# First Fourier axis of a mixing block folded once more: rows s paired with 272 - s, in four regrouped row tiles

## The chip, the cores and the metric

The kernel runs on one core of a Trainium2 chip. The metric is the device time of one execution in microseconds: 313.57 us is the median of 3 runs before the change (313.29 to 314.12). The profile that is shown is of one such execution, with a span of 312.0 us.

## The reference

A cross attention between 512 tokens `x` and 32 state rows (8 heads of 64 columns, batch 8) gives 544 rows of 512 columns for each batch. On these a Fourier mixing block works: the real part of a two-dimensional DFT is added, the rows are normalised, and a two-layer network (512 to 2048 to 512) is applied.

```python
def _attn_ref(x, state):                      # x (8, 8, 512, 64), state (8, 8, 32, 64)
    scores = scale * x @ state^T              # softmax over the 32 states
    xread = softmax(scores) @ state           # 512 rows
    scores2 = scale * state @ x^T             # softmax over the 512 tokens
    sread = softmax(scores2) @ x              # 32 rows
    return concatenate([xread, sread], axis=2)

def _moe_ref(x, w_ch1, w_ch2):                # x (8, 544, 512): heads side by side
    X = np.fft.fft(np.fft.fft(x, axis=1), axis=2)
    u = x + np.real(X)
    un = (u - mean(u)) / sqrt(var(u) + 1e-6)  # over the last axis
    return u + np.maximum(un @ w_ch1, 0) @ w_ch2
```
(shortened)

## The kernel before

The first Fourier axis has 544 rows s. A cosine is the same for s and 544 - s, a sine changes sign, so the kernel adds row 544 - s to row s first, and 288 table rows are left for the matmul (`NM = 288`: outputs 1 to 287 and 0). Rows come as three tiles: rows 1 to 128 and 129 to 256, each with its mirrored partner, and the *low* tile of 32 rows (257 to 287, and 0), which is read by a small attention read of its own. The columns (second axis) are folded twice, which gives four quarters j of 128 columns. The parts that matter, with cuts marked `...`:

```python
def load_x(b):
    if b < 2:                                       # 1 KB pieces: 4 rows of a head
        v = xs.rearrange("p (h r) -> p h r", h=H)
        xb = x[b].rearrange("h (p i) d -> p h (i d)", i=4)
        ...
    # b >= 2: rows by tile, pieces of 64 float32 = 256 bytes
    for ps, si, rows in ((slice(32, 128), 2, xb[288:384]), (slice(0, 128), 0, xb[1:129]),
                         (slice(0, 128), 1, xb[129:257]), (slice(0, 128), 3, xb[384:512]),
                         (slice(0, 31), 2, xb[257:288]), (slice(31, 32), 2, xb[0:1])):
        nc.sync.dma_start(out=v[ps, si], in_=rows)

def xread(c0, rev, name, o, ...):                   # attention read of 128 rows
    # two matmuls of 260 columns on TensorE, then reciprocal and product on VectorE

def low():
    xread(256 - 32 * bq, False, "xlp", XL[pq, 0:512], pq)

def fold_rows(k, eng=nc.vector):
    eng.tensor_add(Sm[:, k], XF[:, k], XR[:, k])                          # L518
    eng.tensor_add(XE[:, k, 0:256], Sm[:, k, 0:256], Sm[:, k, 512:256:-1])  # L519
    eng.tensor_copy(XE[:, k, 256:257], Sm[:, k, 256:257])                 # L520
    yield

def fold():                                         # on VectorE
    next(fold_rows(slice(1, 2) if b < 2 else slice(0, 2)))
    nc.vector.tensor_add(XQ[:, 0], XE[:, :, 0:128], XE[:, :, 256:128:-1]) # L529
    nc.vector.tensor_sub(XQ[:, 1], XE[:, :, 0:128], XE[:, :, 256:128:-1]) # L530
    nc.vector.tensor_copy(XN[:, :, 0:1], XE[:, :, 128:129])
    nc.vector.tensor_sub(XO[:, 0:2, 1:256], Sm[:, :, 1:256], Sm[:, :, 511:256:-1])
    nc.vector.tensor_sub(XQ[:, 2], XO[:, :, 0:128], XO[:, :, 256:128:-1]) # L533
    nc.vector.tensor_add(XQ[:, 3], XO[:, :, 128:0:-1], XO[:, :, 128:256]) # L534

second = [                                          # the reads of a batch, woven into the stream
    lambda: xread(256, True, "xrp", XR[:, 0, 1:513]),
    sread if b < 2 else sread_by_head,              # overwrites XR[0:32, 0]
    None if b > 1 else lambda: (low(), fold_low_early()),
    lambda: xread(0, False, "xfp", XF[:, 0, 0:512], apart=(b == 0)),
    low if b > 1 else lambda: next(fold_rows(slice(0, 1), nc.gpsimd)),
    lambda: xread(128, False, "xfp", XF[:, 1, 0:512], apart=(b == 0)),
    (lambda: (fold_low(True), fold_low(False))) if b > 1 else None,
    lambda: (xread(384, True, "xrp", XR[:, 1, 1:513]), fold()),
]

def over_s(j):                                      # first axis, quarter j of the columns
    p = qt("gp")
    tab = cos if j < 2 else sin
    for c in range(3):                              # three row tiles, 288 outputs
        nc.tensor.matmul(p[:, 0:NM], lhsT=XQ[:, j, c, :], rhs=tab[c],
                         start=(c == 0), stop=(c == 2 and j != 2))
    if j == 2:
        for c in range(3):
            nc.tensor.matmul(p[:, 0:NM], lhsT=XN[:, c, :], rhs=cos[c], start=False, stop=(c == 2))
    ...                                             # copy to G by ScalarE
```

The eight batches overlap: while the network of batch b runs (`layer1` writes `ph`, `layer2` writes `po`), the reads of batch b+1 and then its transform are woven into TensorE's stream at fixed shares of the stretch:

```python
def weave(*streams):    # sorts the steps of all streams by lo + (hi - lo) * (i + 0.5) / len(steps)
...
streams.append((reads_next, 0, 0.34))
streams.append((transform(b + 1), 0.47 if b == 1 else 0.4, 0.77 if b == 3 else 0.8))
```

Each engine works its instructions off in program order. The `warm` matmuls at the start compute nothing that is used.

Of the kernel before, what the change touches and what calls it, by code (L numbers as in the profile page):

```python
# [12 lines left out]
F32 = mybir.dt.float32  # L13
# [17 lines left out]
def kernel(  # L31
# [43 lines left out]
    nc.gpsimd.iota(lt, pattern=[[1, NM]], base=1, channel_multiplier=0)  # L75
# [3 lines left out]
    for hh in range(4):  # L79
        nc.gpsimd.iota(pi_[32 * hh:32 * hh + 32, 2:3], pattern=[[0, 1]], base=257, channel_multiplier=1)  # L80
# [28 lines left out]
    def load_x(b):  # L109
        xs = wk.tile([128, 4 * dm], F32, name="xs", tag="xs")  # L110
        xs_of[b] = xs
        if b < 2:
            v = xs.rearrange("p (h r) -> p h r", h=H)
            xb = x[b].rearrange("h (p i) d -> p h (i d)", i=4)
            n = 2 if b == 0 else 4
            for h in range(0, H, n):
                queue = nc.scalar if b == 0 and h in (0, 4) else nc.sync
                queue.dma_start(out=v[:, h:h + n, :], in_=xb[:, h:h + n, :])
            return
        v = xs.rearrange("p (i h d) -> p i h d", i=4, d=D)  # L120
        xb = x[b].rearrange("h s d -> s h d")
        for ps, si, rows in (
            (slice(32, 128), 2, xb[288:384]),
            (slice(0, 128), 0, xb[1:129]),
            (slice(0, 128), 1, xb[129:257]),
            (slice(0, 128), 3, xb[384:512]),
            (slice(0, 31), 2, xb[257:288]),
            (slice(31, 32), 2, xb[0:1]),
        ):
            nc.sync.dma_start(out=v[ps, si], in_=rows)  # L130

    def cast_x(b, copy=nc.gpsimd.tensor_copy, lo=0, hi=H):
        if b < 2:
            copy(xin_bufs[b % 2][:, :, 1 + D * lo:1 + D * hi].rearrange("p i (h d) -> p h i d", d=D),
                 xs_of[b].rearrange("p (h i d) -> p h i d", i=4, d=D)[:, lo:hi])
        else:
            copy(xin_bufs[b % 2][:, :, 1:513], xs_of[b].rearrange("p (i c) -> p i c", i=4))  # L137
# [38 lines left out]
    CL = singles.tile([128, 4, NM], BF16, name="CL")  # L176
    SL = singles.tile([128, 4, NM], BF16, name="SL")
    cast_x(0, nc.scalar.copy, 0, 2)
    cast_x(0, nc.scalar.copy, 2, 4)
    cast_x(0, lo=4, hi=6)  # L180
    cast_x(0, lo=6, hi=8)

# [10 lines left out]
    XE, XO = singles.tile([128, 3, 257], F32, name="XE"), singles.tile([128, 3, 257], F32, name="XO")  # L193
    XQs, XNs = two("XQ", [128, 4, 3, 128]), two("XN", [128, 3, 128])
# [3 lines left out]
    CT = singles.tile([128, 2, NM], BF16, name="CT")  # L198
    ST = singles.tile([128, 2, NM], BF16, name="ST")
# [4 lines left out]
    cl1 = gen1[:, 2048:2048 + NM // 2].bitcast(BF16)  # L204
    sl1 = gen1[:, 2560:2560 + NM // 2].bitcast(BF16)
# [18 lines left out]
    nc.vector.memset(lt[:, NM - 1:NM], 0)  # L224
    nc.vector.tensor_copy(pf, pi_)
    nc.vector.scalar_tensor_tensor(pf[:, 2:3], in0=pf[:, 2:3], scalar=float(NM), in1=pf[:, 2:3], op0=ALU.is_lt, op1=ALU.mult)
    pn = singles.tile([128, 3], F32, name="pn")
    nc.vector.tensor_scalar(pn, in0=pf[:, 0:3], scalar1=1.0 / Stot, scalar2=None, op0=ALU.mult)
    f1, q1 = turn(NM, Stot, lt, [0, 1, 2], gen1)
# [22 lines left out]
    def sines():  # L252
        w = 2.0 * PI / Stot * shrink
        nc.scalar.activation(CT, q1[:, 0:2, :], AF.Sin, bias=halfpi, scale=-w)
        nc.scalar.activation(ST, f1[:, 0:2, :], AF.Sin, bias=0.0, scale=w)
        nc.scalar.activation(CL[0:32, 0, :], q1[0:32, 2, :], AF.Sin, bias=halfpi[0:32], scale=-w)
        nc.scalar.activation(SL[0:32, 0, :], f1[0:32, 2, :], AF.Sin, bias=0.0, scale=w)

    def low_tables(hh):
        pq = slice(32 * hh, 32 * hh + 32)  # L260
        nc.gpsimd.tensor_copy(CL[pq, hh, :], cl1[pq])
        nc.gpsimd.tensor_copy(SL[pq, hh, :], sl1[pq])

    def more_sines():
        w = 2.0 * PI / dm * shrink
        nc.scalar.activation(TE[:, 0:128], q2_[:, 0:128], AF.Sin, bias=mhalfpi, scale=w)
        nc.scalar.activation(TE[:, 128:256], q2_[:, 0:128], AF.Sin, bias=sg[:, 2:3], scale=sg[:, 3:4])
        nc.scalar.activation(TO[:, 0:128], f2[:, 256:384], AF.Sin, bias=0.0, scale=w)
        nc.scalar.activation(TO[:, 128:256], f2[:, 256:384], AF.Sin, bias=0.0, scale=sg[:, 3:4])
        nc.scalar.activation(TE[:, 256:384], q2_[:, 128:256], AF.Sin, bias=mhalfpi, scale=w)  # L270
        nc.scalar.activation(TE[:, 384:512], q2_[:, 128:256], AF.Sin, bias=sg[:, 2:3], scale=sg[:, 3:4])
        nc.scalar.activation(TO[:, 256:384], f2[:, 128:256], AF.Sin, bias=0.0, scale=w)
        nc.scalar.activation(TO[:, 384:512], f2[:, 128:256], AF.Sin, bias=0.0, scale=sg[:, 3:4])

    def last_sines():
        w = 2.0 * PI / Stot * shrink
        nc.scalar.activation(cl1, q1[:, 2, :], AF.Sin, bias=halfpi, scale=-w)
        nc.scalar.activation(sl1, f1[:, 2, :], AF.Sin, bias=0.0, scale=w)
# [9 lines left out]
    def clears(i):  # L288
        nc.gpsimd.memset(XFs[i][:, :, 512:514], 0.0)
        nc.gpsimd.memset(XRs[i][:, :, 0:514:513], 0.0)  # L290
        nc.gpsimd.memset(XLs[i][:, 512:514], 0.0)
        if i == 0:
            nc.gpsimd.memset(XE[:, 2, :], 0.0)
            nc.gpsimd.memset(XO[:, 2, :], 0.0)
            nc.gpsimd.memset(XO[:, 0:2, 0:257:256], 0.0)
        nc.gpsimd.memset(XNs[i].rearrange("p a b -> p (a b)"), 0.0)

# [6 lines left out]
    nc.gpsimd.memset(CL.rearrange("p a b -> p (a b)").bitcast(F32), 0.0)  # L304
    nc.gpsimd.memset(SL.rearrange("p a b -> p (a b)").bitcast(F32), 0.0)
# [3 lines left out]
    def more_loads():  # L309
        nc.gpsimd.tensor_copy(gate[:, 0:1], XQs[0][:, 3, 0, 0:1])  # L310
# [7 lines left out]
    def last_loads():  # L318
        for hh in range(1, 4):
            low_tables(hh)  # L320
# [37 lines left out]
    def attend(b):  # L358
# [4 lines left out]
        XQ, XN = XQs[b % 2], XNs[b % 2]  # L363
# [19 lines left out]
        def turn_x(g):  # L383
# [5 lines left out]
            for k in range(2):  # L389
                for si in range(4):  # L390
                    o = k * 512 + si * 128
                    nc.tensor.transpose(p[:, o:o + 128], xin[:, si, 1 + 128 * (2 * g + k):129 + 128 * (2 * g + k)], ident)
            (nc.vector.tensor_copy if g == (b == 0) else nc.scalar.copy)(
                xT[:, 2 * g:2 * g + 2, :], p.rearrange("p (a b) -> p a b", b=S))
# [18 lines left out]
        def scores_t(g):  # L413
            p = qt("eTp")
            for i in range(4):
                x0 = 128 * i
                for cols, rows in ((slice((i - 1) % 4, 285 if i == 0 else 288, 4), slice(x0 + (i == 0), x0 + 72)),
                                   (slice(287, 288), slice(0, 1)) if i == 0 else (None, None),
                                   (slice(291 - i, S, 4), slice(x0 + 127, x0 + 71, -1))):
                    for hp in range(2 if cols else 0):  # L420
                        nc.tensor.matmul(p[:, cols], lhsT=sT[:, 2 * g + hp, :], rhs=xT[:, 2 * g + hp, rows],  # L421
                                         start=(hp == 0), stop=(hp == 1))
            nc.scalar.activation(ET[:, g, :], p, AF.Exp, scale=scale)
# [16 lines left out]
        def turn_scores(g):  # L440
            p = qt("eTp")
            for si, o, rhs in ((0, 0, ident), (1, 128, ident), (2, 256, ident[:, 0:32]),
                               (2, 416, mirror[:, 0:96]), (3, 288, mirror)):
# [62 lines left out]
        def low():  # L506
            xread(256 - 32 * bq, False, "xlp", XL[pq, 0:512], pq)

        def fold_low(even, eng=nc.vector):
            if even:  # L510
                eng.tensor_add(XE[pq, 2, 0:256], XL[pq, 0:256], XL[pq, 512:256:-1])
                eng.tensor_copy(XE[pq, 2, 256:257], XL[pq, 256:257])
            else:
                eng.tensor_sub(XO[pq, 2, 1:256], XL[pq, 1:256], XL[pq, 511:256:-1])


        def fold_rows(k, eng=nc.vector):
# [3 lines left out]
            yield  # L521

        def fold_low_early():
            fold_low(True, nc.gpsimd)
            fold_low(False, nc.gpsimd)

        def fold():
            next(fold_rows(slice(1, 2) if b < 2 else slice(0, 2)))
            nc.vector.tensor_add(XQ[:, 0], XE[:, :, 0:128], XE[:, :, 256:128:-1])  # L529
            nc.vector.tensor_sub(XQ[:, 1], XE[:, :, 0:128], XE[:, :, 256:128:-1])  # L530
            nc.vector.tensor_copy(XN[:, :, 0:1], XE[:, :, 128:129])
            nc.vector.tensor_sub(XO[:, 0:2, 1:256], Sm[:, :, 1:256], Sm[:, :, 511:256:-1])
            nc.vector.tensor_sub(XQ[:, 2], XO[:, :, 0:128], XO[:, :, 256:128:-1])  # L533
            nc.vector.tensor_add(XQ[:, 3], XO[:, :, 128:0:-1], XO[:, :, 128:256])  # L534
# [349 lines left out]
```

The softmax here doesn't subtract the row's maximum and nothing guards it: scores larger than these inputs give would overflow.

## Time and profile before

| what | value |
|---|---|
| time | 313.57 us (313.29 to 314.12) |
| span of the profile | 312.0 us |
| granted TensorE clock, mean | 0.999 |
| gp matmuls, first axis (lines 599 and 603), 288 columns | 120 in the program |
| xlp matmuls (low read), 260 columns | 16 in the program |
| one gp after another | 0.122 us |
| reads and folds of one batch on VectorE | about 171 to 176.4 us for batch 5 |

TensorE (PE) is nearly always busy. Where such an engine waits, its next instruction is named in the list of waits; where it doesn't wait, the order of its stream tells how far ahead of their use the operands are made. Lengths of single matmuls in the trace include their way through the array, so what one costs in a stream is read from the distance of the starts. In lines of the timeline the columns are start, length, engine, line, operation, output and inputs, count, and in brackets idle time and what ended it.

### The profile page before, as it was taken

How to read it: one execution, taken by the hardware profiler on the slowest of the kernel's cores; microseconds unless marked ns; L12 is line 12 of the kernel's file. 1: busy time of each engine (PE TensorE's matmuls, PEld its weight loads, DVE VectorE, ACT ScalarE, POOL GpSimd, SP SyncE). 2: the span in 40 equal slices, each digit the busy share in tenths (PEclk: the TensorE clock that was granted, in tenths of full speed). 3: DMA queues.
4: the chain of work that ended last, by engine and by line, in shares of the span. 5: the costliest groups of instructions: out<-in, count | busy, mean ns of one | idle time of the engine just before them, and what ended most of it. 6: DMA issues, size and time to landing. Idle time of an engine off the chain costs nothing.

```text
span 312.0 us, 5999 instructions
## 1 busy us (share of the span) xinstructions
PE 298.4 (96%) x2316; PEld 172.5 (55%) x2348; DVE 183.5 (59%) x441; ACT 134.9 (43%) x265; POOL 73.0 (23%) x168
## 2 busy tenths in 40 slices
PE   5988999999999999999999999999999999999995
PEld 5867996544554545456545554455445544555443
DVE  8687782877778484864727684686569563100112
ACT  5598664735533543334533434234423333333300
POOL 4969590440240040300500024002200131000000
PEclk9999999999999999999999999999999999999999
DMA  7997999358456756297533577631332034302055
GB/s 235 186 186 141 172 147 163 94 105 177 75 110 98 147 103 137 67 120 114 141 84 67 127 120 163 134 86 50 83 71 67 36 80 97 78 34 67 36 133 136
DMA packets 108052, 34.86 MB, mean 112 GB/s; under 512 B 97400, under 2 KB 103800, under 8 KB 108024
## 3 DMA queue, kind: packets, MB, share of 16 engines
q1 hardware_dynamic: 98840, 28.72, 45.5%
q0 software_dynamic: 4224, 4.19, 9.1%
q10 hardware_dynamic: 4960, 1.57, 2.0%
q8 instruction: 18, 0.29, 0.4%
q14 instruction: 10, 0.08, 0.1%
HBM read 22.41 MB, written 14.02 MB: 117 GB/s over the span
## 4 chain that ended last, share of the span: by engine, by line
PE 79%; DVE 13%; DMA 2%; issue 2%; ACT 2%; POOL 0%; ACTq 0%; DVEq 0%; POOLq 0%
PE po L789 32%; PE ph L724 30%; PE gp L599 4%; PE ph L734 3%; DVE U L569 2%; DVE st L335 2%; DMA xs<-in_x_dram 1%; PE eTp L421 1%; PE yp L565 1%; DVE ot L755 1%; PE xfp L457 1%; PE xrp L457 1%; PE yp L564 1%; PE gp L603 1%; PE esp L432 1%
## 5 line engine op out<-in xcount | busy, mean ns | idle before, releaser
L789 PE MATMUL po<-w,hT 128*128 128x512 bf16 x476 | 122.0, 379 | 1.5 <-issue 0.8
L726 ACT ACTIVATE hT<-ph 128x512 bf16<-128x512 f32 x112 | 66.9, 597 | 124.8 <-PE ph L724 122.7
L724 PE MATMUL ph<-unT,w 128*128 128x512 bf16 x437 | 114.1, 379 | 1.0 <-DVE ot L755 0.3
L724 PEld LDWEIGHTS <-w 128*128 128x128 bf16 x576 | 51.2, 98 | 47.9 <-issue 0.8
L789 PEld LDWEIGHTS <-hT 128*128 128x128 bf16 x496 | 47.1, 98 | 45.3
L755 DVE SCALAR_TENSOR_TENSOR ot<-po,rstd,U 128x512 f32<-128x512 f32 (+2 forms) x33 | 24.2, 732 | 52.9 <-PE po L789 44.9
L609 POOL COPY GL<-G 128x128 bf16<-128x128 bf16 x8 | 2.3, 290 | 113.7 <-ACT G L607 113.7
L569 DVE TENSOR_TENSOR U<-yp,XR 128x512 f32<-128x512 f32 x16 | 10.9, 682 | 27.0 <-PE yp L565 27.0
L335 DVE BATCH_NORM_STATS2 st<-U 128x6 f32<-128x512 f32 x32 | 21.8, 682 | 0.1
L342 POOL TENSOR_TENSOR rstd<-rstd,mhalf 128x1 f32<-128x1 f32 x34 | 21.0, 619 | 2.7
L341 POOL TENSOR_TENSOR rstd<-mv,epst 128x1 f32<-128x1 f32 x34 | 6.8, 200 | 62.5 <-DVE mv L337 62.5
L607 ACT CAST G<-gp 128x288 bf16<-128x288 f32 x31 | 12.0, 398 | 10.6 <-PE gp L603 5.7
L734 PE MATMUL ph<-unT,w 128*128 128x128 bf16 x256 | 16.1, 219 | 0.5 <-ACT unT L645 0.5
L809 PE MATMUL warm<-ident 128*128 128x128 bf16 x144 | 12.4, 234 | 3.6 <-POOL ident masks.py:199 3.3
L734 PEld LDWEIGHTS <-w 128*128 128x128 bf16 x256 | 15.0, 98 | 0.8 <-issue 0.6
L599 PEld LDWEIGHTS <-XQ 128*128 128x128 bf16 x96 | 8.8, 98 | 8.8 <-DVE XQ L529 2.5
L633 DVE TENSOR_SCALAR ub<-U,mv 128x512 bf16<-128x512 f32 x24 | 12.3, 511 | 1.3 <-DVE mv L337 0.5
L809 PEld LDWEIGHTS <-ident 128*128 128x128 bf16 x144 | 10.4, 107 | 4.6 <-POOL ident masks.py:199 3.3
L137 POOL CAST xin<-xs 128x2048 bf16<-128x2048 f32 x6 | 11.3, 1889 | 3.2 <-PE tp L642 3.2
L457 PEld LDWEIGHTS <-ET 128*128 128x128 bf16 x80 | 7.0, 98 | 9.1 <-DVE XF L466 1.8
L466 DVE TENSOR_TENSOR XR<-xrp,rs 128x512 bf16<-128x512 f32 x16 | 11.1, 695 | 1.0 <-POOL XR L290 0.5
L736 ACT ACTIVATE hT<-ph 128x512 bf16<-128x512 f32 x16 | 9.4, 598 | 4.2 <-PE ph L734 4.0
(183 smaller groups left out, 351.6 us busy)
## 6 DMA issues: line engine op xcount, KB each, us to landing
xs<-in_x_dram SPq DMA_DIRECT2D x20, 256.0 KB, 4.8
w<-in_moe_w_ch_dram POOLq DMA_DIRECT2D x8, 512.0 KB, 10.6
out_dram<-ot SPq DMA_DIRECT2D x15, 256.0 KB, 3.5
r_dram<-ot SPq DMA_DIRECT2D x14, 256.0 KB
out_dram<-r_dram SPq DMA_DIRECT2D x14, 256.0 KB, 3.7
xs<-in_x_dram SPq DMA_DIRECT2D x6, 192.0 KB
xs<-in_x_dram SPq DMA_DIRECT2D x2, 512.0 KB
xs<-in_x_dram ACTq DMA_DIRECT2D x2, 256.0 KB
```

The costliest lines, as they stand in the source:

```text
L335: nc.vector.bn_stats(st6, u)
L342: nc.gpsimd.tensor_tensor(rstd, rstd, mhalf, op=ALU.pow)
L457: nc.tensor.matmul(ph[:, 0:260], lhsT=ET[:, g, c0:c0 + 128], rhs=rhs, start=True, stop=True)
L569: nc.vector.tensor_add(u.rearrange("p (k r) -> p k r", r=2), p.rearrange("p (r k) -> p k r", r=2)[:, 0:u.shape[1] // 2, :], x.rearrange("p ...
L599: nc.tensor.matmul(p[:, 0:NM], lhsT=XQ[:, j, c, :], rhs=tab[c], start=(c == 0), stop=(c == 2 and j != 2))
L633: nc.vector.tensor_scalar(t, in0=ud, scalar1=mv[:, 0:1], scalar2=None, op0=ALU.subtract)
L724: nc.tensor.matmul(ph[:, o:o + n], lhsT=w1[:, c, f * 128:(f + 1) * 128], rhs=un_of[key][:, c, :], start=(c == 0), stop=(c == DC - 1))
L726: nc.scalar.activation(hT[:, per * i:per * i + per, :].rearrange("p a b -> p (a b)"), ph, AF.Relu, scale=-1.0 if key in flipped else 1.0)
L734: nc.tensor.matmul(ph[:, o:o + 128], lhsT=w1[:, c, f * 128:(f + 1) * 128], rhs=un_of[key][:, c, 128 * r:128 * r + 128], start=(c == 0), st ...
L755: nc.vector.scalar_tensor_tensor(ot[:, cols], in0=po_of[i][:, 0:cols.stop - cols.start], scalar=rstd, in1=u[:, cols], op0=ALU.mult, op1=AL ...
L789: nc.tensor.matmul(po_of[i], lhsT=h_of[key][:, f, i * 128:(i + 1) * 128], rhs=w2[:, f, :], start=(f == 0), stop=(f == FC - 1))
L809: nc.tensor.matmul(t[:, 0:128], lhsT=ident, rhs=ident, start=(i == 0), stop=(i == n - 1))
```

## The change

It uses one more symmetry of the first axis: 544 = 2 x 272, so a table entry for row 272 - s is that for row s, up to a sign that depends only on whether the output is odd or even. Rows 1 to 128 are paired with 271 to 144 by a sum and a difference; each of these serves only one half of the outputs. The 288 outputs stand as 144 odd and 144 even ones. A matmul then has one row tile and 144 columns instead of two row tiles and 288 columns. Rows 129 to 143, 272, 0 and their partners stay unfolded: they form the low part of 32 rows. They now lie in the fourth tile of x, so that one ordinary read (`read_low`) gives them with the last full tile, and GpSimd copies them aside (`XT`) before the state rows overwrite them. Batch 0 skips the new fold and uses four operands with a negated table `TN`. The load of batches 0 and 1 takes the same row order as the others.

The diff, cut to its core (cuts marked `...`; iotas, table phases and clears follow the new order of rows):

```diff
     def load_x(b):
-        if b < 2:
-            ... # 1 KB pieces
         for ps, si, rows in (
-            (slice(32, 128), 2, xb[288:384]),
             (slice(0, 128), 0, xb[1:129]),
-            (slice(0, 128), 1, xb[129:257]),
-            (slice(0, 128), 3, xb[384:512]),
-            (slice(0, 31), 2, xb[257:288]),
-            (slice(31, 32), 2, xb[0:1]),
+            (slice(0, 128), 1, xb[144:272]),
+            (slice(0, 128), 2, xb[273:401]),
+            (slice(32, 128), 3, xb[416:512]),
+            (slice(0, 15), 3, xb[129:144]),
+            (slice(16, 31), 3, xb[401:416]),
+            (slice(15, 16), 3, xb[0:1]),
+            (slice(31, 32), 3, xb[272:273]),
         ):
-            nc.sync.dma_start(out=v[ps, si], in_=rows)
+            queue = nc.scalar if b == 0 and si in (0, 2) else nc.sync
+            queue.dma_start(out=v[ps, si], in_=rows)
...
     def sines():
-        ... # CT, ST over two row tiles, CL, SL for the low rows
+        nc.scalar.activation(TC, q1, AF.Sin, bias=halfpi, scale=-w)
+        nc.scalar.activation(TS, f1, AF.Sin, bias=0.0, scale=w)
+        nc.scalar.activation(TS[32:64, 1, :], q1[32:64, 1, :], AF.Sin, bias=halfpi[32:64], scale=-w)
+    def sines_turned():
+        nc.gpsimd.tensor_scalar(TN[:, 0:144], in0=TC[:, 0, 0:144], scalar1=-1.0, ...)
+        nc.gpsimd.tensor_scalar(TN[:, 144:288], in0=TS[:, 0, 144:288], scalar1=-1.0, ...)
...
     def scores_t(g):                # batches 0 and 1
-        ... # 9 pieces of 1 to 72 columns, 2 matmuls each
+        for cols, rows in (4 pieces of 128, 128, 160 and 96 columns):
+            ... # 2 matmuls each
...
-        def low():
-            xread(256 - 32 * bq, False, "xlp", XL[pq, 0:512], pq)
+        def read_low():
+            xread(384, True, "xrp", XR[:, 0, 1:513])
+            nc.gpsimd.tensor_copy(XT, XR[0:32, 0, :])
+        def fold_low():
+            ... # 7 GpSimd operations on 32 rows: XT -> XEl, XOl -> XQl
...
         def fold():
-            next(fold_rows(slice(1, 2) if b < 2 else slice(0, 2)))
-            nc.vector.tensor_add(XQ[:, 0], XE[:, :, 0:128], XE[:, :, 256:128:-1])
-            ... # XQ[:, 1], XN, XO, XQ[:, 2], XQ[:, 3], three row tiles each
+            fold_rows(slice(1, 2) if b < 2 else slice(0, 2))
+            t = XQ0 if b == 0 else XW              # XW: float32, two row tiles
+            nc.vector.tensor_add(t[:, 0], XE[:, :, 0:128], XE[:, :, 256:128:-1])
+            nc.vector.tensor_sub(t[:, 1], XE[:, :, 0:128], XE[:, :, 256:128:-1])
+            ... # XN: a sum and a difference of one column; one column of XQl
+            nc.vector.tensor_sub(XO[:, :, 1:256], Sm[:, :, 1:256], Sm[:, :, 511:256:-1])
+            nc.vector.tensor_sub(t[:, 2], XO[:, :, 0:128], XO[:, :, 256:128:-1])
+            nc.vector.tensor_add(t[:, 3], XO[:, :, 128:0:-1], XO[:, :, 128:256])
+            if b:
+                o = XQ.rearrange("p (g j c) -> p g j c", g=2, j=4)
+                nc.vector.tensor_add(o[:, 0], XW[:, :, 0], XW[:, :, 1])
+                nc.vector.tensor_sub(o[:, 1], XW[:, :, 0], XW[:, :, 1])
...
         second = [
-            ... # as above
+            read_low,
+            sread if b < 2 else lambda: xread(0, False, "xfp", XF[:, 0, 0:512]),
+            fold_low,
+            (lambda: xread(0, False, "xfp", XF[:, 0, 0:512], apart=(b == 0))) if b < 2 else sread_by_head,
+            (lambda: fold_rows(slice(0, 1), nc.gpsimd)) if b < 2 else None,
             lambda: xread(128, False, "xfp", XF[:, 1, 0:512], apart=(b == 0)),
-            (lambda: (fold_low(True), fold_low(False))) if b > 1 else None,
-            lambda: (xread(384, True, "xrp", XR[:, 1, 1:513]), fold()),
+            None,
+            lambda: (xread(256, True, "xrp", XR[:, 1, 1:513]), fold()),
         ]
...
         def over_s(j):
             p = qt("gp")
-            ... # 3 (j = 2: 6) matmuls of 288 columns
+            tab = TC if j < 2 else TS
+            for q in range(2):                     # 144 odd, then 144 even outputs
+                cols = slice(144 * q, 144 * q + 144)
+                steps = []
+                for t, kind in ((tab, j), (TC, 4)) if j == 2 else ((tab, j),):
+                    plus = (t is TC) == (q == 1)
+                    if b == 0:
+                        ... # two operands, the second with TN or the table
+                    else:
+                        g = 0 if plus else 1
+                        steps.append((XN[:, g, :] if kind == 4 else Xg[:, g, j, :], t[:, 0, cols]))
+                steps.append((XQl[:, j, :], tab[:, 1, cols]))
+                for n, (w, t) in enumerate(steps):
+                    nc.tensor.matmul(p[:, cols], lhsT=w, rhs=t, start=(n == 0), stop=(n == len(steps) - 1))
...
         def done():
-            ... # tiles 128*k + 1
+            dst = {(0, 0): out[b, 1:129, :], (1, 1): out[b, 273:401, :], (0, 1): (b, 0, 543), (1, 0): (b, 1, 271)}[k, r]
+            nc.scalar.copy(XLs[g4][32 * bq:32 * bq + 32, 0:512], XTs[b % 2][:, 512:0:-1])
...
+    sin_table()                                    # loads the sine table before the first reads
-    weave((warmed(r0, 4), 0, 1), ([sines], 0.25, 0.25), ([more_sines], 0.3, 0.3), ([lambda: warm(44)], 1, 1))
+    weave((warmed(r0, 4), 0, 1), ([sines], 0.25, 0.25), ([more_sines], 0.3, 0.3), ([sines_turned], 0.6, 0.6),
+          ([lambda: warm(44)], 1, 1))
```

The shares at which reads and transforms are woven into the stream are not changed.

## The prediction

> **What bounds the kernel now.** I read the first and fourth parts of the page first: who is busy, and whose work the chain that ended last consists of.
>
> ```profile
> PE 298.4 (96%) x2316; PEld 172.5 (55%) x2348; DVE 183.5 (59%) x441; ACT 134.9 (43%) x265; POOL 73.0 (23%) x168
> PE 79%; DVE 13%; DMA 2%; issue 2%; ACT 2%; POOL 0%; ACTq 0%; DVEq 0%; POOLq 0%
> ```
>
> TensorE is the bound: anything taken from its stream should come off the time, and any wait put into its stream is added. The 13% of VectorE lies in the first 25 us and in a few spots where TensorE waits for it. So next I read TensorE's stream (timeline) around the first-axis transform of one late batch, batch 5, and VectorE's stream in the same stretch. Columns: start us, length us, engine, line, operation, tiles, count.
>
> ```profile
> 170.71 0.39 PE L457 MATMUL xrp<-stb,ET 128*128 128x260 bf16 x2
> 170.94 1.03 PE L724 MATMUL ph<-unT,w 128*128 128x512 bf16 x4
> 171.80 1.03 PE L789 MATMUL po<-w,hT 128*128 128x512 bf16 x4
> 172.66 1.03 PE L724 MATMUL ph<-unT,w 128*128 128x512 bf16 x4
> 173.53 1.03 PE L789 MATMUL po<-w,hT 128*128 128x512 bf16 x4
> 174.39 0.41 PE L599 MATMUL gp<-CT,XQ 128*128 128x288 bf16 x2
> ```
>
> ```profile
> 171.13 0.21 DVE L465 RECIPROCAL rs<-xrp 128x8 f32<-128x8 f32 x1 [0.17 <-PE xrp L457]
> ...
> 172.83 0.69 DVE L519 TENSOR_TENSOR XE<-Sm 128x512 f32<-128x512 bf16 x1
> ...
> 173.64 0.56 DVE L529 TENSOR_TENSOR XQ<-XE 128x384 bf16<-128x384 f32 x1
> 174.12 0.55 DVE L530 TENSOR_TENSOR XQ<-XE 128x384 bf16<-128x384 f32 x1
> ...
> 174.65 0.68 DVE L532 TENSOR_TENSOR XO<-Sm 128x510 f32<-128x510 bf16 x1
> 175.37 0.56 DVE L533 TENSOR_TENSOR XQ<-XO 128x384 bf16<-128x384 f32 x1
> 175.85 0.55 DVE L534 TENSOR_TENSOR XQ<-XO 128x384 bf16<-128x384 f32 x1
> ```
>
> The reader is to see how tight this is. The last attention read (xrp) starts at 170.71. TensorE then has 16 matmuls of 512 columns, and reaches the transform (gp) at 174.39, 3.68 us later. VectorE starts on xrp 0.42 us after it began and finishes the first quarter of XQ at 174.20. So the transform finds its first operand 0.2 us before it is needed, and the other three quarters are made while it runs: the last one ends at 176.40, two us after gp began. Looking the same up for every late batch, gp starts 4.16, 3.86, 4.57, 3.68, 3.68 and 3.67 us after xrp (batches 2 to 7). There is almost no slack, and XQ is used piecewise.
>
> **What the Trainium skill says.** "TensorE: Matmul & The Clock Gate", section "Wait — 56ns, not 53.3ns?": a warm matmul of N columns follows the one before after N/2.4 ns plus about 2.5 ns. The trace agrees: 112 matmuls of 128 columns in 6.25 us are 55.8 ns each, and the 288-column ones come every 0.122 us. Its Part 1 on the clock gate says that an idle window of some 3.4 us halves the clock; no stretch of this trace shows it (granted clock 0.999). "VectorE: DVE Perf Modes", section "Mode 2×_2P": a float32 tensor_tensor stays at one element per cycle. The trace agrees: 384 float32 elements come every 0.48 us, while 1028 bf16 ones take 0.69. "DMA: Bandwidth & Descriptors", section on why a DMA increments its semaphore by 16: a transfer is spread over the largest k up to 16 that divides its slowest dimension, so 31 rows run on one engine and 15 rows on 15. The trace fits: the end of the load with 31 rows runs at 17 GB/s with 0.09 of the DMA engines busy (57 to 59 us).
>
> **TensorE's saving.** First axis, batches 1 to 7: before, 15 matmuls of 288 columns, 15 x 0.1226 = 1.84 us. After, 4 outputs x 2 halves x 2 operands plus 2 Nyquist ones are 18 matmuls of 144 columns at 144/2.4 + 2.5 = 62.5 ns, 1.13 us. That is 0.71 us less for a batch. Batch 0 keeps the unfolded operands: 28 matmuls of 144, 1.75 us, nothing gained. The separate low read (xlp, two matmuls of 260) goes: 0.22 us for a batch. For batches 0 and 1 the transposed scores need 8 matmuls of 128 columns on average instead of 18 small ones: 0.94 becomes 0.45 us, twice a batch. From batch 1 on, all this sits on the bound: batch 1 gives 0.71 + 0.22 + 0.98 = 1.9 us, batches 2 to 7 give 6 x 0.93 = 5.6 us.
>
> **VectorE's new wait, the main term.** The folds no longer write XQ quarter by quarter. They write float32 XW, and only two last operations of 512 elements make XQ: first the sum, then the difference. The program order of the changed kernel has the first gp matmul of batches 1 to 7 read the difference, so it waits for all of the fold. From the start of the first fold operation (173.64 above), with the steps of like operations of this trace: two of 256 elements at 0.345; three tiny ones at 0.1; XO 0.72; XW 0.345, and 0.46 for the one that the next depends on; the sum 0.61; the difference 0.69 to its end. Together 3.82, plus 0.06 to TensorE: 3.88 us. The first fold operation itself starts 2.93 us after xrp. It can hardly start earlier: the low work that leaves VectorE was done by then in batches 4 to 7, and frees 0.3 to 0.6 us only in batches 3 and 2. So gp can start 2.93 + 3.88 = 6.8 us after xrp. The program order still puts the same 16 matmuls (3.67 us) between the two, and in batch 4 the same low-row ones besides. TensorE therefore stands still for about 3.1 us in a batch. Against the gaps of before the addition is 2.64 + 2.94 + 2.23 + 3.12 + 3.12 + 3.13 = 17.2 us for batches 2 to 7. In batch 1 there are 6.3 us of other matmuls after xrp and the fold is some 0.4 us shorter there, so nothing is added.
>
> **The start.** x of batches 0 and 1 now comes in 256-byte pieces rather than 1 KB ones. In this trace 1 KB pieces ran at 343 GB/s (4 to 8 us) and 256-byte pieces at about 228 (26 to 30 us): 1.05 MB take 1.5 us longer. As the landing of the last part lagged, I put the last cast 0.9 us later. GpSimd's stream then decides, and this is its stretch before:
>
> ```profile
> 14.07 1.28 POOL L162 CAST stb<-gen 32x128 bf16<-32x128 f32 x4
> 15.45 0.66 POOL L511 TENSOR_TENSOR XE<-XL 32x256 f32<-32x256 bf16 x1
> ...
> 16.83 1.15 POOL L518 TENSOR_TENSOR Sm<-XF,XR 128x514 bf16<-128x514 bf16 x1
> 18.05 0.67 POOL L519 TENSOR_TENSOR XE<-Sm 128x256 f32<-128x256 bf16 x1
> ```
>
> ```profile
> 14.04 2.56 ACT L487 ACTIVATE XR<-srp,rcs 32x64 bf16<-32x64 f32 x8 [0.97 <-DVE rcs L478]
> 16.62 1.28 ACT L254 ACT_TABLE_LOAD   x1
> 17.91 0.78 ACT L254 ACTIVATE CT<-gen,halfpi 128x576 bf16<-128x576 f32 x1
> ```
>
> After: the memsets of CL, SL and of a part of XE and XO go (1.6 us), one of XQl comes (0.3); with the later cast the state blocks end at about 14.9. Only then can GpSimd copy the low rows out of XR (0.6), and only then may ScalarE overwrite them: XR 15.5 to 18.1 instead of 14.04 to 16.6. The sine table is loaded before, so the tables are ready at 19.4. In GpSimd's program order the two negated tables stand ahead of its row fold, so it goes on with them at 19.4 (0.6), then Sm 1.15, XE 0.67, a copy 0.2: 22.0. VectorE can begin its folds at 22.0 instead of 19.64. Its shorter folds give back 0.4, TensorE may be throttled a little after such a pause (an estimate of 0.6 by the clock-gate section): 2.6 us for the start. The 0.98 us of shorter scores and the removed low read are already in these dates.
>
> **Sum.** 313.57 + 2.6 - 1.9 - 5.6 + 17.2 = 325.9; I say 326.
>
> **Rivals.** (1) *The saving simply shows*: TensorE is at 96%, 7.5 us leave it, and the waits are hidden: 306 to 309 us. For it speaks the first part of the page; against it the two timelines above, where the transform begins 0.2 us after its first operand and 2 us before its last. (2) *Only part of the wait appears*: VectorE might start on xrp earlier, or run the two new operations closer together, so that about 2 us a batch remain: 320 us. Against it: in batches 4 to 7 VectorE already waits for xrp. (3) *The pauses also throttle TensorE*: they are near the 3.4 us of the skill's window. A halved clock for one window after each of six pauses costs up to 1.7 us each: 332 us or more. The pauses are just short of the window, so I take this as the upper tail. (4) *Loads become faster*: 15 rows over 15 engines remove the slow end of each load of x. No TensorE wait for a later load is in the list of waits, so this gives nothing except room at the start.
>
> **Range and chances.** The main term rests on a count of instructions and on durations of like ones; an error of 0.5 us in the pause is 3 us in all. The start is uncertain by 2 us either way. Throttling pulls upwards. That makes 318 to 332. Slower by over 2% means above 319.8: chance 0.87. Within 2%: 0.10, when pauses are below 2 us. Faster by over 2%, below 307.3: 0.03, rival (1).
>
> **What would show it right or wrong.** In the changed profile the waits of TensorE should list gp waiting for VectorE's last XQ operation, some 17 to 19 us in all over six batches, the longest near 3.1; xrp to gp should be about 6.8 us in batches 2 to 7. The group of gp matmuls of 144 columns should come every 62 ns, and xlp be gone. The first gp should start near 22.5 instead of 20.25. If gp follows xrp within 4 us, or VectorE's fold ends within 5 us of xrp, the main step is wrong. If the granted clock falls clearly below 0.99, rival (3) is in play.

## The result and the profile after

The changed kernel takes 336.97 us (median of 4 runs, 336.05 to 338.16), the kernel before 313.8 in the same series: a ratio of 1.074, with a 95% interval of 1.071 to 1.077. The prediction said 326, range 318 to 332. The direction and the cause that it named were right, and the size was 11 us too small, which puts the result above the range.

First the page of the changed kernel: the busy times, and the row of the TensorE clock over 40 slices of 8.4 us.

```profile
PE 298.3 (89%) x2295; PEld 170.9 (51%) x2326; DVE 177.8 (53%) x438; ACT 140.4 (42%) x267; POOL 97.0 (29%) x221
...
PEclk9998999997999799999999999997999799999999
```

TensorE is now 89% busy instead of 96%. Its busy time is the same although it has less work, and the clock row shows why: four slices in the body stand at 7, where the row of before is 9 throughout. The mean granted clock fell from 0.999 to 0.974. Next the list of what TensorE waited for (us in total, times, longest):

```profile
PE gp L605 <- DVE XQ L529: 17.3, 6, 3.0
PE gp L605 <- DVE XQ L515: 3.7, 1, 3.7
...
PE xfp L445 <- DVE XR L454: 2.2, 5, 1.0
```

The first line is the new wait: six times 2.1 to 3.0 us, at the last operation of the fold (L529 here). The second is the start, the third a wait in the reads that before amounted to 0.2 us here and there. This is TensorE's stream around the transform of batch 3:

```profile
102.28 0.39 PE L445 MATMUL xrp<-stb,ET 128*128 128x260 bf16 x2
...
105.09 1.03 PE L788 MATMUL po<-w,hT 128*128 128x512 bf16 x4
109.16 0.24 PE L605 MATMUL gp<-TC,XQ 128*128 128x144 bf16 x1 [3.04 <-DVE XQ L529]
109.23 0.23 PE L605 MATMUL gp<-TC,XQl 128*128 128x144 bf16 x1
...
110.87 0.32 PE L605 MATMUL gp<-TC,XQ 128*128 128x144 bf16 x1
110.99 0.32 PE L605 MATMUL gp<-TC,XQl 128*128 128x144 bf16 x1
...
111.35 1.89 PE L788 MATMUL po<-w,hT 128*128 128x512 bf16 x4
```

And VectorE's in the same stretch:

```profile
105.21 0.43 DVE L515 TENSOR_TENSOR XW<-XE 128x256 f32<-128x256 f32 x1
...
107.01 0.42 DVE L524 TENSOR_TENSOR XW<-XO 128x256 f32<-128x256 f32 x1
107.36 0.42 DVE L525 TENSOR_TENSOR XW<-XO 128x256 f32<-128x256 f32 x1
107.81 0.69 DVE L528 TENSOR_TENSOR XQ<-XW 128x512 bf16<-128x512 f32 x1
108.42 0.68 DVE L529 TENSOR_TENSOR XQ<-XW 128x512 bf16<-128x512 f32 x1
```

The last fold operation ends at 109.10, gp starts at 109.16. In all batches from 2 to 7 gp starts 6.87 or 6.88 us after xrp. The gp matmuls first follow each other after 62 to 67 ns. From 110.87 on they take 120 ns, and a group of four 512-column matmuls takes 1.89 us instead of 1.03: TensorE runs at half its clock. The stretches of the same execution show it directly. The columns are the stretch, its length, the busy times of PE, PEld, DVE, ACT and POOL, then the granted clock, the DMA share and GB/s:

```profile
107.00:108.00 1.00, 0.00 (x0) 0.00 (x0) 0.95 (x3) 0.00 (x0) 0.00 (x0) 1.00 0.56 89
108.00:109.00 1.00, 0.00 (x0) 0.00 (x0) 1.00 (x2) 0.00 (x0) 0.00 (x0) 1.00 1.37 259
109.00:110.00 1.00, 0.84 (x6) 0.47 (x7) 0.10 (x1) 0.33 (x1) 0.00 (x0) 0.84 1.07 294
110.00:111.00 1.00, 0.78 (x4) 0.42 (x4) 0.00 (x0) 0.15 (x1) 0.00 (x0) 0.50 1.28 252
...
113.00:114.00 1.00, 1.00 (x6) 0.47 (x5) 0.72 (x1) 0.00 (x0) 0.00 (x0) 0.96 1.19 193
```

Here the clock is full during the pause, and is halved for some 3.4 us *after* it, when TensorE has work again. This follows the pauses of batches 2, 3, 6 and 7, and the one at the start.

### The profile page after: what moved, and what is told of

Same layout as the page of the kernel before. It is cut to its first block, busy times and chain, and to the rows that moved or that the text cites. A ratio compares the mean times of both kernels' runs of the same rounds, so it can differ in the third digit from the quotient of the medians.

```text
span 334.3 us, 6025 instructions
## 1 busy us (share of the span) xinstructions
PE 298.3 (89%) x2295; PEld 170.9 (51%) x2326; DVE 177.8 (53%) x438; ACT 140.4 (42%) x267; POOL 97.0 (29%) x221
## 4 chain that ended last, share of the span: by engine, by line
PE 73%; DVE 16%; POOL 4%; issue 3%; DMA 1%; SPq 1%; ACT 1%; DVEq 0%; ACTq 0%; POOLq 0%
PE po L788 29%; PE ph L724 28%; PE gp L605 4%; PE ph L734 3%; DVE XR L454 2%; DVE XO L523 1%; DVE Sm L508 1%; DMA xs<-in_x_dram 1%; DVE XE L509 1%; DVE XQ L529 1%; PE xfp L445 1%; PE yp L559 1%; PE yp L560 1%; PE po L780 1%; PE xrp L445 1%
## 5 line engine op out<-in xcount | busy, mean ns | idle before, releaser
L788 PE MATMUL po<-w,hT 128*128 128x512 bf16 x480 | 125.0, 385 | 1.3 <-issue 0.6
L726 ACT ACTIVATE hT<-ph 128x512 bf16<-128x512 f32 x112 | 66.9, 597 | 122.6 <-PE ph L724 118.6
L606 ACT CAST G<-gp 128x288 bf16<-128x288 f32 x31 | 14.6, 481 | 29.9 <-PE gp L605 29.9
L564 DVE TENSOR_TENSOR U<-yp,XR 128x512 f32<-128x512 f32 x16 | 10.9, 682 | 27.8 <-PE yp L560 27.8
L605 PE MATMUL gp<-TC,XQ 128*128 128x144 bf16 x34 | 6.7, 251 | 21.0 <-DVE XQ L529 17.3
L605 PEld LDWEIGHTS <-XQ 128*128 128x128 bf16 x72 | 7.6, 112 | 27.3 <-DVE XQ L529 20.0
L132 POOL CAST xin<-xs 128x2048 bf16<-128x2048 f32 (+1 forms) x9 | 14.4, 1604 | 8.1 <-DMA xs<-in_x_dram 7.8
L496 POOL COPY XT<-XR 32x514 bf16<-32x514 bf16 x8 | 4.8, 603 | 30.9 <-DVE XR L454 30.8
L454 DVE TENSOR_TENSOR XR<-xrp,rs 128x512 bf16<-128x512 f32 x16 | 11.1, 695 | 1.0 <-POOL XR L285 0.4
```

The costliest lines, as they stand in the source:

```text
L132: copy(xin_bufs[b % 2][:, lo:hi, 1:513], xs_of[b].rearrange("p (i c) -> p i c", i=4)[:, lo:hi])
L454: nc.vector.tensor_tensor(ov, in0=p[ps, :, 0:256].rearrange("p g (h d) -> p g h d", d=D), in1=rs[ps].unsqueeze(3).to_broadcast([n, 2, 4, D ...
L605: nc.tensor.matmul(p[:, cols], lhsT=w, rhs=t, start=(n == 0), stop=(n == len(steps) - 1))
L606: (nc.vector.tensor_copy if b == 0 and j == 3 else nc.scalar.copy)(G[:, j, :].rearrange("p (i q) -> p q i", q=2), p[:, 0:NM].rearrange("p ...
L726: nc.scalar.activation(hT[:, per * i:per * i + per, :].rearrange("p a b -> p (a b)"), ph, AF.Relu, scale=-1.0 if key in flipped else 1.0)
L788: nc.tensor.matmul(po_of[i], lhsT=h_of[key][:, f, i * 128:(i + 1) * 128], rhs=w2[:, f, :], start=(f == 0), stop=(f == FC - 1))
```

## The experiments

Theory: TensorE's stream is stopped at gp by a fold that has to be complete, and most of what is missing in the prediction is the halved clock behind the pauses. Rivals: other new waits are the cost; a pause is made up elsewhere; the added work costs wherever it stands. Unless something else is said, the edits are on the changed kernel, and all times are medians beside runs of the kernel before on the same chip (313.2 to 313.8 us).

**e1: work for nothing in the pause**

```diff
         def over_s(j):
+            if b >= 2 and j == 0:
+                t = qt("fill")
+                for i in range(42):
+                    nc.tensor.matmul(t[:, 0:128], lhsT=ident, rhs=ident, ...)
```

> The changed kernel with 42 matmuls of 128 columns, used for nothing, ahead of the first gp matmul of batches 2 to 7 (2.3 us of work in the 3 us pause). Theory (pause plus throttling): gp still starts 6.9 us after xrp, but TensorE is not idle, so the half-clock stretches after the pauses of batches 2, 3, 6 and 7 (3.4 us at half clock, 1.7 us lost each) go: about 330 us, clock 0.99. Rival (the pauses and other new waits are the whole cost): 337 us as before.

Measured: 329.95 us, ratio 1.052 (1.049 to 1.055), clock 0.995; gp 6.88 to 6.91 us after xrp. Around the transform of batch 3 the stretches of this run now read:

```profile
106.00:107.00 1.00, 1.00 (x21) 1.00 (x19) 0.97 (x3) 0.00 (x0) 0.00 (x0) 1.00 0.12 25
107.00:108.00 1.00, 0.83 (x15) 0.66 (x12) 0.97 (x3) 0.00 (x0) 0.00 (x0) 1.00 1.07 169
...
109.00:110.00 1.00, 0.95 (x8) 0.64 (x8) 0.00 (x0) 0.63 (x2) 0.00 (x0) 1.00 1.00 251
110.00:111.00 1.00, 1.00 (x8) 0.41 (x6) 0.03 (x1) 0.83 (x2) 0.00 (x0) 1.00 1.24 253
```

gp comes no earlier in its stretch, its waits in the list fall from 17.3 to 3.5 us because the work for nothing fills them, and the kernel is 7.0 us faster by doing more. Those 7 us were the halved clock, separated from the waiting.

**e2: the transform later in the stream**

```diff
-            streams.append((transform(b + 1), 0.47 if b == 1 else 0.4, 0.77 if b == 3 else 0.8))
+            streams.append((transform(b + 1), 0.57 if b == 1 else 0.5, 0.82 if b == 3 else 0.85))
```

> The changed kernel with the transform woven in 0.1 of the stretch later (0.5 instead of 0.4; batch 2 0.57 instead of 0.47; ends moved by 0.05). Theory: TensorE has 3 us of network matmuls more before gp, so the 17 us of pauses and the throttling behind them (about 7 us) go: 313 us, or less. Rival: the normalised rows then come too late for the next network, the wait moves there: above 322 us.

Measured: 318.23 us, ratio 1.015 (1.012 to 1.018), clock 0.994. The place in the stream is worth 18.7 us. The 313 us were missed: waits of 2.9 us at gp remain (the network matmuls come in lumps of four; batch 2 still pauses 1.1 us), and the wait in the reads grew to 3.7 us.

**e3: no second fold in any batch**

```diff
-            t = XQ0 if b == 0 else XW
+            t = XQ.rearrange("p (j k c) -> p j k c", j=4, k=2)
-            if b:                       # the two operations that make XQ from XW
+            if False:
...
-                    if b == 0:          # two operands and the negated table
+                    if True:
```

> The changed kernel without the second fold in any batch: batches 1 to 7 work as batch 0 does, with two operands and the negated table, and XQ written quarter by quarter. Theory: 28 instead of 18 gp matmuls cost 0.62 us a batch (4.4 us), but the 17 us of pauses and about 7 us of throttling go: 317 us. Rival (pauses come from elsewhere: the low fold on GpSimd, the order of reads): above 330 us.

Measured: 316.81 us, ratio 1.010 (1.008 to 1.013). gp is back at 3.67 us after xrp (4.57 in batch 4). The low fold on GpSimd and the order of reads, which are kept here, do not make the pauses.

**e4: the wait alone, in the kernel before**

```diff
+            if b < 2:
                 nc.vector.tensor_add(XQ[:, 0], XE[:, :, 0:128], XE[:, :, 256:128:-1])
...
             nc.vector.tensor_add(XQ[:, 3], XO[:, :, 128:0:-1], XO[:, :, 128:256])
+            if b >= 2:
+                nc.vector.tensor_add(XQ[:, 0], XE[:, :, 0:128], XE[:, :, 256:128:-1])
```

> The kernel before with one thing changed: in batches 2 to 7 the first quarter of XQ is made last. Theory: gp waits for the whole fold, some 5.8 us after xrp instead of 3.7 to 4.6: 11 us of pauses, 325 us; pauses of 2.1 us are too short to throttle, clock 0.99. Rival (a pause of TensorE is made up elsewhere): 314 us.

Measured: 326.56 us, ratio 1.041 (1.036 to 1.045). Not one instruction is added; one operation of VectorE stands five operations later, and it costs 13 us. The list of waits of this run has

```profile
PE gp L602 <- DVE XQ L537: 11.5, 6, 2.5
```

so a pause of TensorE is not made up elsewhere. The longest pause (2.5 us, batch 2) was followed by half a clock from 77.6 to 81.1 us; the others, 1.0 to 2.2 us, were not. That is the step over the expected 325: two runs with a granted clock of 1.00 took 324.9 and 325.8 us, two with 0.995 and 0.990 took 327.3 and 327.8.

**e5: the second fold ahead of the column folds**

```diff
-                nc.vector.tensor_add(o[:, 0], XW[:, :, 0], XW[:, :, 1])     # at the end
-                nc.vector.tensor_sub(o[:, 1], XW[:, :, 0], XW[:, :, 1])
+                nc.vector.tensor_add(SG[:, 0], Sm[:, 0], Sm[:, 1])          # right after Sm
+                nc.vector.tensor_sub(SG[:, 1], Sm[:, 0], Sm[:, 1])
+                # XE, XO from SG; XQ[:, :, j] quarter by quarter from these
```

> The changed kernel with the second fold moved ahead of the column folds in batches 1 to 7: sum and difference of the two row tiles are made first (two operations of 514 elements into float32), and XQ is again written quarter by quarter. Same arithmetic, same gp matmuls, same place in the stream. Theory (what costs is that the whole fold stands ahead of the first gp): gp about 4.9 us after xrp, pauses of 1.2 us instead of 3.0, too short to throttle: 337 - 11 - 7 = 319 us. Rival (the added VectorE work costs, wherever it stands): 330 us or more.

Measured: 316.11 us, ratio 1.009 (1.007 to 1.010). VectorE in batch 3 of this run, with xrp at 98.03:

```profile
100.16 0.69 DVE L519 TENSOR_TENSOR SG<-Sm 128x514 f32<-128x514 bf16 x1
100.77 0.69 DVE L520 TENSOR_TENSOR SG<-Sm 128x514 f32<-128x514 bf16 x1
...
102.30 0.42 DVE L526 TENSOR_TENSOR XQ<-XE 128x256 bf16<-128x256 f32 x1
```

The same sums and differences in another place: gp can start 4.74 us after xrp instead of 6.88, the pauses are 0.9 us, and no halved clock follows them. In batches 2 to 7 it was not the added arithmetic that cost, but that all of the fold stood ahead of the first gp. A part of the 3 us below the expected 319 comes from the start (see e8): the gp of batch 1 begins at 50.43 us instead of 51.29.

**e6: the start**

```diff
-            nc.gpsimd.tensor_copy(XT, XR[0:32, 0, :])
+            (nc.vector if b == 0 else nc.gpsimd).tensor_copy(XT, XR[0:32, 0, :])
...
-            fold_rows(slice(1, 2) if b < 2 else slice(0, 2))
+            fold_rows(slice(1, 2) if b == 1 else slice(0, 2))   # GpSimd's part goes in batch 0
```

> The changed kernel with only the start altered: in batch 0 VectorE, not GpSimd, copies the low rows aside and folds the first row tile. Theory (GpSimd's queue of low copy, low fold, negated tables and row fold sets the first gp): first gp near 20.8 us instead of 23.1, its pause under 2 us, so no throttling there: 333 us. Rival (the later landing of x in 256-byte pieces sets it): first gp stays above 22.5, 336 to 337 us.

Measured: 334.65 us, ratio 1.067 (1.063 to 1.071). First gp at 20.70 us instead of 23.12; the last cast of x came as late as ever (8.94). So it was GpSimd's queue, which in the changed kernel looks like this:

```profile
15.38 0.60 POOL L496 COPY XT<-XR 32x514 bf16<-32x514 bf16 x1
...
19.47 0.58 POOL L260 TENSOR_SCALAR TN<-TC 128x144 bf16<-128x144 bf16 x1
20.04 0.56 POOL L261 TENSOR_SCALAR TN<-TS 128x144 bf16<-128x144 bf16 x1
20.58 1.15 POOL L508 TENSOR_TENSOR Sm<-XF,XR 128x514 bf16<-128x514 bf16 x1
...
22.42 0.18 POOL L510 CAST XE<-Sm 128x1 f32<-128x1 bf16 x1
```

VectorE was idle from 19.2 to 22.6 us, waiting for that last copy.

**e7 and e9: all corrections together**

e7 has e5, e6, the second read one place later in batches 2 to 7 (`[read_low, fold_low, xfp, sread_by_head, ...]`), and the transform at 0.44 (batch 2: 0.51). e9 lets VectorE copy the low rows aside in batch 1 as well:

```diff
-            (nc.vector if b == 0 else nc.gpsimd).tensor_copy(XT, XR[0:32, 0, :])
+            (nc.vector if b < 2 else nc.gpsimd).tensor_copy(XT, XR[0:32, 0, :])
```

> The changed kernel with the row tiles folded first, the start on VectorE, the second read one place later in the order of reads, and the transform woven in 0.04 of the stretch later. Theory: pauses and throttling gone, the saving of TensorE work (1.9 us in batch 1, 0.93 us in each later batch) shows: 306 to 309 us, faster than the kernel before. Rival (the work that was moved costs as much as was saved): 313 us or more.

> The kernel with all four corrections (309.3 us), with VectorE copying the low rows aside in batch 1 too. In that kernel TensorE waited 3.2 us in batch 1: GpSimd's copy stood behind a cast that waited for the load of batch 2. Theory: that wait goes, about 306 us. Rival (the wait moves to the next use of the loads): 309 us.

Measured: e7 309.29 us, ratio 0.988 (0.984 to 0.992); e9 304.93 us, ratio 0.973 (0.970 to 0.975), with a clock of 0.999. e9 is faster than both kernels. In e7 one wait of 3.2 us stood in batch 1, because the copy was behind a cast in GpSimd's queue that waited for a load; e9 has it no more. Page and TensorE stream of e9 (batch 5):

```profile
PE 292.4 (96%) x2322; PEld 166.9 (55%) x2322; DVE 179.1 (59%) x433; ACT 139.4 (46%) x267; POOL 94.4 (31%) x214
```

```profile
164.52 0.39 PE L445 MATMUL xrp<-stb,ET 128*128 128x260 bf16 x2
...
168.20 1.03 PE L727 MATMUL ph<-unT,w 128*128 128x512 bf16 x4
169.26 0.24 PE L608 MATMUL gp<-TC,XQ 128*128 128x144 bf16 x1
```

TensorE is at 96% as before the change, with 6 us less to do. Five groups of network matmuls instead of four stand between xrp and gp, and the list has no wait at gp after the start.

**e10 and e11: what of this is the fold, and what the place**

e10 is e9 without the second fold (as e3); e11 is e9 with the transform at 0.4 and 0.47 again.

> The kernel of 304.9 us with all corrections, but without the second fold: every batch works as batch 0 does, with two operands and the negated table. It tells what the fold itself is worth once it stands in the right place. Theory (each gp matmul taken away counts fully, TensorE being the bound): 10 matmuls of 62.5 ns more in each of batches 1 to 7, 4.4 us: 309.3 us. Rival (the fold saves nothing that shows; the gain comes from the start and the order of reads): 305 us.

> The kernel of 304.9 us with all corrections, but with the transform at its old place in the stream (0.4 and 0.47 of the stretch). Theory: gp can start 4.74 us after xrp and TensorE arrives after 3.67 (batch 4: 4.57), so pauses of about 1 us in five batches and 0.2 in one come back, 5 us in all, too short to throttle: 310 us. Rival (the place was not what mattered): 305 us.

Measured: e10 308.15 us, ratio 0.983 (0.981 to 0.986); e11 309.20 us, ratio 0.986 (0.984 to 0.988). The second fold is worth about 3.2 us once it stands right (4.4 were worked out), and 0.04 of the stretch in the place about 4.3. Most of what the fold lacks can be seen in the streams: with the same five groups between, gp follows xrp after 4.54 us in five batches of e10, but after 4.74 or 4.75 in e9. There gp still comes 0.2 us late in each of the five, 1.0 us in all.

**e8: 32 bytes**

```diff
-    XW = singles.tile([128, 4, 2, 128], F32, name="XW")
+    XWp = singles.tile([128, 1032], F32, name="XWp")        # 1024 of them are used
```

> The changed kernel with one tile (XW) 32 bytes longer on each partition, so that later tiles lie 32 bytes further; nothing else. The first load of x was slower in the changed kernel (the packets of its second half took about 25 ns) than in the two kernels whose fold tile has another size (18 ns). Theory (the place of the tiles in SBUF decides it): the last cast of x starts near 7.6 us instead of 8.9, first gp near 21.8 instead of 23.1, 335 to 336 us. Rival (chance from run to run): 337 us, cast at 8.9.

Measured: 333.92 us, ratio 1.067 (1.062 to 1.072); the last cast of x starts at 7.43 us instead of 8.87, first gp at 21.68 instead of 23.12. e5 and e7, with a fold tile of another size, have this cast at 7.40 and 7.39, and e6, with the old one, at 8.94. The stretches of the load, first the changed kernel, then e8:

```profile
5.00:6.00 1.00, 1.00 (x13) 1.00 (x11) 0.97 (x3) 0.31 (x2) 0.00 (x0) 1.00 1.35 218
7.00:8.00 1.00, 0.76 (x11) 0.59 (x9) 0.00 (x0) 0.80 (x1) 0.61 (x1) 1.00 1.25 182
```

```profile
5.00:6.00 1.00, 1.00 (x12) 1.00 (x10) 0.96 (x3) 0.87 (x2) 0.00 (x0) 1.00 1.28 287
7.00:8.00 1.00, 1.00 (x12) 0.85 (x10) 0.00 (x0) 0.79 (x1) 0.70 (x3) 1.00 0.62 142
```

From 5 to 6 us the load runs at 287 GB/s instead of 218. All runs agree: those with the tile of the changed kernel (it, e1, e2, e3, e6) have 217 to 222 GB/s there, those with a longer one (e5, e7 to e11) 284 to 287. So the 1.4 us at the first gp depend on where the tiles lie. Only 0.5 of them are left at the gp of batch 1 (50.76 us against 51.29); in a read of that batch TensorE now waits 1.4 us, which it does not in the changed kernel. The rest of the difference is the clock: the spans of the two profiles are 2.2 us apart, and e8 has three halved stretches in the body instead of four, which is 1.7 us. Why 32 bytes matter stays open.

## Why the prediction fell short

- **The wait at gp: right.** Worked out were 6.8 us from xrp to gp and 17.2 us more waiting; the trace has 6.87 or 6.88 us, which is 17.7 us more in all than before, and 17.3 us of waiting at gp where before 0.3 stood. The steps of the fold, summed from like operations, were right to 0.1 us. e4 and e5 show from both sides that the last operation's place is the cause.
- **The saving: right to 0.3 us.** The gp matmuls come every 62 to 67 ns, xlp is gone. From the gp of batch 1 to the end, e9 needs 256.8 us (303.1 - 46.3) and the kernel before 263.5 (312.0 - 48.5): 6.7 us less. The prediction's terms for that stretch give 7.0 (0.71 and 5.6, and the 0.7 by which gp came later than 3.67 us after xrp in batches 2 and 3 of before).
- **The throttling: the step that failed.** The sum held an estimate of 0.6 us, for the start alone, and the text said of rival (3) "The pauses are just short of the window, so I take this as the upper tail". It took a pause to be harmless while it is shorter than the window. The clock was halved after four of the six pauses of the profile, and e1 measures 7.0 us for it, where the sum had none. This is about two thirds of the 11 us. The price that rival (3) named for one pause, up to 1.7 us, was about right (7.0 for the four of the profile).
- **The start: 2.6 us expected for it, of which batch 1 should have given 1.2 back before its gp.** The gp of batch 1 came 2.8 us later instead of 1.4. The chain through GpSimd was the named one (first gp 23.12 against "near 22.5"), and e6 confirms it. What was missing: the clock is halved there for a full 3.4 us (24.3 to 27.8 us), by estimate 1.7 us lost instead of 0.6, and the first gp comes 0.6 us later than said, to which the slower load that e8 found adds.
- **The reads: not in the sum.** The new order of reads brings a read of xfp at most one group of network matmuls (0.86 us) after xrp, while VectorE still empties the only buffer of that kind (`psX`, one buffer). That is the 2.2 us of the third line in the list of waits, 1.0 of it here in batch 2, where xfp follows xrp directly. In e7 and e9, which read in another order, 0.2 us of it are left:

```profile
65.98 0.39 PE L445 MATMUL xfp<-stb,ET 128*128 128x260 bf16 x2 [1.03 <-DVE XR L454]
```

Together 7.0 + 1.4 + 2.2, and 0.5 from the 0.08 us in each of six pauses, are 11.1 us; the prediction fell short by 11.0. That this closes to 0.1 us is partly luck, since the runs of the changed kernel alone are 2 us apart.

## What to carry to other kernels

When an operation is moved or split, ask first what the next engine needs of it first, and make that first: with two operations of 0.7 us at the end of the fold TensorE waited 17 us, with the same arithmetic at its beginning about 5. In e4 the pauses of the engine that is the bound were paid in full (11.5 us of waits, 13 us of time), and TensorE may pay for a pause twice, once by waiting and once by a halved clock after it. When a tight place is changed, its place in the woven stream has to be set anew.

## What was not expected of the hardware

- A pause need not be as long as the throttle's window. The Trainium skill, "TensorE: Matmul & The Clock Gate", in "HAM oscillation", states the rule as no idle gaps above some 3.4 us. Here pauses of 3.04 us were followed by the halved clock in 11 of 15 cases (the profiles of the changed kernel, e6 and e8), one of 2.5 us was as well (e4), and none of three of 2.1 us. The halving begins between 0.9 us before and 1.3 us after the end of the pause and lasts 3.4 us, once 6.8 (e6).
- Which pauses are hit can be read from the traces. In each profile the changes of the granted clock lie on a grid of 3.413 us: the halvings of the changed kernel begin at 24.34, 78.95, 109.67, 225.73 and 263.27 us, at distances of 16, 9, 34 and 11 times 3.413. What tells hit from miss is how long TensorE stood idle within the one step of this grid just before. Three steps of the changed kernel, and as the last line one of e8 (the second number is the length, the third the time that PE was busy):

```profile
75.54:78.95 3.41, 0.37 (x2) 0.00 (x1) 3.26 (x9) 0.60 (x1) 0.00 (x0) 1.00 0.57 139
259.86:263.27 3.41, 1.27 (x11) 0.86 (x13) 1.99 (x4) 0.48 (x2) 0.00 (x0) 1.00 0.00 0
184.77:188.18 3.41, 1.54 (x8) 0.49 (x5) 3.28 (x11) 0.60 (x1) 0.00 (x0) 1.00 0.70 83
106.65:110.06 3.41, 1.44 (x13) 0.97 (x14) 1.88 (x4) 0.60 (x2) 0.00 (x0) 1.00 1.01 216
```

  The first two, idle for 3.0 and 2.1 us, were followed by the halved clock; the last two, idle for 1.9 and 2.0 us, were not. In the twelve profiles with a halving (the kernel before has its only one at 311.2 us, behind TensorE's last work; counted from the first change of the clock, at 7 to 13 us), 25 full-clock steps were followed by it, and in these TensorE was idle for at least 1.99 us; in the other 1042 it was idle for at most 1.97. So some 2 us within one step were enough here (an estimate, as the ends of matmuls are modelled). How a pause of 3.04 us falls on the grid differs from run to run: that of batch 3 was hit in the changed kernel and e6 and missed in e8.
- A tile that is 32 bytes longer moved the first load's rate at 5 to 6 us from 218 to 287 GB/s.
